# Score matmuls of two query tiles issued as one burst, with the second tile's PSUM banks read one and two steps later

## The chip, the core and the metric

The kernel runs on one core of one Trainium2 chip. The metric is the device time of one execution in microseconds (us). Before the change the median of three runs is 1856.72 us (1854.34 to 1858.67). A difference of 0.2% (3.7 us) is about what a measurement of this kernel can tell from no change.

Engines are named as the profile names them: PE is TensorE (PEld is its weight load), DVE is VectorE, ACT is ScalarE, POOL is GpSimd, SP is SyncE, which only issues DMAs here (SPq in the timeline).

## The reference

Inputs are `q`, `k`, `v` of shape (8 batches, 8 heads, 576 rows, 64), and the weights `moe_w_ch1` (512 x 2048) and `moe_w_ch2` (2048 x 512), all float32.

```python
scores = scale * np.matmul(q, k.transpose(0, 1, 3, 2))          # 576 x 576 per head
kth = np.partition(scores, -32, axis=-1)[..., -32:-31]          # 32nd largest of each row
scores = np.where(scores >= kth, scores, -1e9)
attn = softmax(scores); attn_out = attn @ v
x = attn_out.transpose(0, 2, 1, 3).reshape(8, 576, 512)
u = x + np.real(fft(fft(x, axis=1), axis=2))                    # FNet mix
un = (u - mean(u)) / sqrt(var(u) + 1e-6)                        # over the 512 channels
out = u + np.maximum(un @ w_ch1, 0) @ w_ch2
```

## The kernel before

**Work units.** Two heads of a batch make a pair, so there are 32 pairs, four to a batch (`NPB = 4`). A pair has nine items, numbered r = 0 to 8 here: `IN_PAIR = [(0, 0), (0, 1), (1, 0), (1, 1), (4, None), (2, 0), (2, 1), (3, 0), (3, 1)]`, each a query tile t of 128 rows and a head e. Item 4 holds the two heads' last 64 rows together. The 288 items follow each other; item i is worked on in step i of one long loop, which is written out when the kernel is built. Within an engine the instructions run in the order in which this loop issues them, and engines meet only at semaphores. The loop goes through the items as a software pipeline. In step i

- PE makes the scores of item i + 3 (`scores`), ACT copies them from PSUM to a tile `S`;
- DVE finds the 32 largest of each row (`top_ops`: four MAX8 and three MATCH_REPLACE8 of 128 x 576), the last two rounds of item i and the first two of item i + 1;
- POOL makes two bounds from them (`nt`, L434); one step later ACT and POOL form the mask (`mask`, L452 and L455), ACT takes the exponential (`expo`, L463);
- two steps later ACT splits the result into 16-bit planes (`plane`, L476), and SP writes them to DRAM (L489, L492); SP reads them back transposed into a tile `PT` (`turn`, L510), and `attend` (L568) multiplies `PT` with v on PE: the first three tiles of a pair in the step of the next pair's r = 0, the other two in that of its r = 3.

This way through DRAM (`by_dma`) is taken in pairs 4 to 30 except pair 7. In the first three pairs of each such batch the attention output is turned by DMA as well (`out_by_dma`).

**Scores of one tile, both heads.** An item of head 0 brings both heads' scores. With D = 64 the two heads lie on partitions 0 to 63 and 64 to 127, so the two matmuls `sp` (L401, 64 rows, 512 keys) use different row halves of PE. The last 64 keys of both heads come from one more matmul of the whole array, `sp_t` (L371), against a small tile `kt`. ACT empties these with two copies of 128 x 512 (L404) and two of 128 x 64 (L375, called tail copies here). In the trace a float32 matmul is two MATMUL instructions, so a tile's scores are four `sp` and two `sp_t` MATMULs. In a step whose item i + 3 has r = 2, 5 or 7 the scores are the first PE work of the step; for r = 0 they are the last of the step's listed work. Steps for r = 1, 3, 6 and 8 have no scores.

**PSUM.** Eight banks: `ps_s` two (tag "sp", the `sp` matmuls), `ps_t` two (tag "tp": `sp_t` and the transposes `prep` of q and k, L308), `ps_o` one, `ps_m` three (the MLP and the Fourier matmuls). Tiles of one tag take its banks in turn, so a `tp` tile waits until ACT has emptied the one before the last.

**What else PE does.** The Fourier mix of a finished batch (`yp` L789, `mp` L846 and L850, `tpu` L915) and its MLP in units of about 2 us: `hp` (L1000, first layer), `cp` (L1027, L1066) and, from the second batch on, a product with seven instead of eight block products (`cv`, `cw`, L1197), which needs sums of hidden blocks from POOL (L1142) and other parts of w2 fetched by SP in the middle of it (`bring`, L943, 512 KB each). A planner spreads these units over the steps: `level` finds a common step length, and after each listed piece of a step `some` issues units while `room`, the step's share less `fixed_cost(i)`, allows it. So `fixed_cost` moves MLP units, with their DMAs and POOL sums, between steps, and does not change their number.

```python
t += {0: 1.04, 1: 0.3, None: 0.9}[items[i + 3][2]]
if by_dma(i + 3) and items[i + 3][2] is not None:
    t += -0.3 if items[i + 3][2] else 0.3
```

## Time and profile before

| | us |
|---|---|
| median of three runs | 1856.72 |
| lowest, highest | 1854.34, 1858.67 |
| the profiled execution, its own time | 1856.44 |
| its span (what the profile shows) | 1854.0 |
| PE busy | 1685.3 (91%) |
| DVE busy | 1569.5 (85%) |
| ACT busy | 1299.3 (70%) |
| POOL busy | 942.7 (51%) |

The span is 2.4 us shorter than the execution's own time. The last MAX8 starts at 1645.8 us; what follows is the end of the last batch, in which PE does the Fourier mix and the MLP. DVE begins pair 20 at 1034.3 us and pair 24 at 1232.7 us: a whole batch in the middle takes some 198 us, of which DVE is busy in 190 and PE in 195.

A timeline line reads: start, duration, engine, line, operation, output <- inputs, tensor types, and how many instructions were merged into it; in brackets the idle time of the engine before it and what ended that.

### The profile page before, as it was taken

Reading aid. Unit: us, or ns where it says so; the run is one execution under the profiler, and the core shown is the slowest. Engines: PE = TensorE matmul, PEld = TensorE weight load, DVE = VectorE, ACT = ScalarE, POOL = GpSimd, SP = SyncE. Lnnn points to the kernel's source line nnn. Section 1 sums busy time; section 2 is a strip of 40 time slices with the busy share of each in tenths; the row PEclk is TensorE's granted clock in tenths of the full one; section 3 lists DMA queues with packets and bytes.
Section 4 is the critical chain, followed back from the end, with each engine's and each line's share of the span. In section 5 each row is a group of like instructions: output and inputs, shape, how many; then the busy total and the mean of one; then the engine's idle time right before and its main releaser. Section 6 shows DMA issues by size and latency. Waiting matters only on the chain.

```text
span 1854.0 us, 26945 instructions
## 1 busy us (share of the span) xinstructions
PE 1685.3 (91%) x8029; PEld 1077.7 (58%) x8029; DVE 1569.5 (85%) x3247; ACT 1299.3 (70%) x3116; POOL 942.7 (51%) x1341
## 2 busy tenths in 40 slices
PE   5676699789899899999999999999999999999999
PEld 3343365356455665557565765667565756676677
DVE  7999989888989999998999999999999899834010
ACT  6878659567698777877798788877887778642100
POOL 4768744454654565446654566355645554350012
PEclk8778799889899999999999999999999999999999
DMA  5334116761467955679557955687567745630051
GB/s 169 105 89 114 26 42 175 184 175 45 114 147 172 242 152 135 152 192 220 120 152 169 253 138 141 155 233 182 121 158 207 210 116 151 167 90 6 6 173 57
DMA packets 562609, 262.24 MB, mean 141 GB/s; under 512 B 433568, under 2 KB 552480, under 8 KB 562464
## 3 DMA queue, kind: packets, MB, share of 16 engines
q1 hardware_dynamic: 561696, 260.32, 54.8%
q8 instruction: 64, 1.05, 0.2%
q14 instruction: 81, 0.66, 0.1%
q10 hardware_dynamic: 768, 0.21, 0.0%
HBM read 93.63 MB, written 90.93 MB: 100 GB/s over the span
## 4 chain that ended last, share of the span: by engine, by line
PE 54%; DVE 13%; POOL 10%; ACT 9%; issue 6%; DMA 6%; SPq 2%; POOLq 0%; DVEq 0%
PE hp L1000 19%; PE cp L1027 6%; DVE m L425 6%; PE o L568 6%; DVE wk L427 6%; PE sp L401 4%; POOL wk L455 4%; PE cv L1197 3%; PE cw L1197 3%; PE yp L789 3%; PE cp L1066 2%; DMA PT<-planes 2%; ACT wk L452 2%; DMA planes<-wk 2%; PE sp_t L371 1%
## 5 line engine op out<-in xcount | busy, mean ns | idle before, releaser
L455 POOL TENSOR_TENSOR wk<-S,wk 128x576 f32<-128x576 f32 x288 | 407.7, 1416 | 495.6 <-ACT wk L452 490.7
L425 DVE MAX8 m<-wk 128x8 f32<-128x576 f32 x864 | 627.2, 750 | 6.6
L1000 PE MATMUL hp<-unT,w 128*128 128x256 f32 (+1 forms) x2048 | 525.6, 410 | 4.9 <-ACT unT L918 3.6
L1000 PEld LDWEIGHTS hp<-unT,w 128*128 128x128 f32 x2048 | 383.5, 192 | 114.1 <-issue 9.4
L427 DVE MATCH_REPLACE8 wk<-m,wk 128x576 f32<-128x576 f32 x576 | 427.7, 742 | 0.0
L476 ACT COPY wk<-S 128x576 uint16<-128x576 uint16 x468 | 289.8, 671 | 0.0
L452 ACT ACTIVATE wk<-S,nt 128x576 f32<-128x576 f32 x288 | 223.5, 776 | 84.5 <-POOL nt L434 83.0
L1027 PE MATMUL cp<-w,hT 128*128 128x512 f32 x512 | 234.6, 599 | 0.0
L425 DVE MAX8 m<-S 128x8 f32<-128x576 f32 x288 | 213.9, 743 | 24.0 <-ACT S L375 24.0
L463 ACT ACTIVATE S<-wk,nt 128x576 f32<-128x576 f32 x234 | 184.9, 790 | 52.0 <-POOL wk L455 50.8
L1004 ACT ACTIVATE hT<-hp 128x320 f32<-128x320 f32 (+1 forms) x256 | 103.2, 412 | 161.3 <-PE hp L1000 160.3
L427 DVE MATCH_REPLACE8 wk<-m,S 128x576 f32<-128x576 f32 x288 | 213.7, 742 | 0.3 <-issue 0.3
L568 PE MATMUL o<-PT,v 128*64 128x256 f32 (+3 forms) x1440 | 196.3, 417 | 7.6 <-DMA PT<-planes 5.5
L401 PE MATMUL sp<-kT,qT 64*128 64x512 f32 (+1 forms) x528 | 170.5, 674 | 12.9 <-ACT means L1391 5.7
L404 ACT COPY S<-sp 128x512 f32<-128x512 f32 (+1 forms) x264 | 141.8, 587 | 30.6 <-PE sp L401 29.9
L568 PEld LDWEIGHTS o<-PT,v 128*64 128x64 f32 x1440 | 115.1, 154 | 82.1 <-issue 23.1
L1027 PEld LDWEIGHTS cp<-w,hT 128*128 128x128 f32 x512 | 94.1, 193 | 90.4 <-issue 89.7
L1142 POOL TENSOR_TENSOR hT<-hT 128x512 f32<-128x512 f32 x64 | 81.0, 1272 | 117.9 <-ACT hT L1004 77.3
L1197 PE MATMUL cw<-w,hT 128*128 128x256 f32 x448 | 107.0, 388 | 13.8 <-ACT ct L1167 7.4
L434 POOL TENSOR_TENSOR nt<-m,cc 128x2 f32<-128x2 f32 x288 | 59.9, 208 | 115.0 <-DVE m L425 110.1
L371 PEld LDWEIGHTS sp_t<-kt,qT 128*128 128x128 f32 x320 | 51.2, 195 | 113.5 <-issue 67.2
L1197 PEld LDWEIGHTS cw<-w,hT 128*128 128x128 f32 x448 | 83.4, 192 | 31.4 <-ACT ct L1167 9.7
(162 smaller groups left out, 2129.7 us busy)
## 6 DMA issues: line engine op xcount, KB each, us to landing
planes<-wk SPq DMA_DIRECT2D x208, 288.0 KB, 2.8
w<-w_parts SPq DMA_DIRECT2D x82, 512.0 KB, 4.9
space<-in_moe_w_ch_dram SPq DMA_DIRECT2D x32, 512.0 KB, 3.6
nat<-in_q_dram SPq DMA_DIRECT2D x128, 64.0 KB, 2.3
v<-in_v_dram SPq DMA_DIRECT2D x64, 128.0 KB, 3.2
out_dram<-x SPq DMA_DIRECT2D x32, 256.0 KB, 2.6
nat<-in_k_dram SPq DMA_DIRECT2D x62, 128.0 KB, 3.2
planes<-wk SPq DMA_DIRECT2D x52, 144.0 KB, 2.6
```

The costliest lines, as they stand in the source:

```text
L401: nc.tensor.matmul(sp[r], lhsT=qT[hd, q_cols], rhs=kT[hd, :], start=True, stop=True)
L404: nc.scalar.copy(out=s_t[r, keys], in_=sp[r])
L425: ops.append(lambda src=src, m8=m8: nc.vector.max(out=m8, in_=src))
L427: ops.append(lambda src=src, m8=m8: nc.vector.match_replace(w, m8, src, NEG))
L452: nc.scalar.activation(out=w, in_=Ssb[i], func=AF.Relu, scale=-FAR, bias=Nt[i][:, 1:2])
L455: nc.gpsimd.tensor_tensor(out=w, in0=Ssb[i], in1=w, op=ALU.subtract)
L463: nc.scalar.activation(out=Ssb[i] if by_dma(i) else w, in_=w, func=AF.Exp, bias=Nt.pop(i)[:, 0:1], accum_out=den_t[pair % 3][:, c:c + 1],)
L476: nc.scalar.copy(out=words[:, half, :], in_=src[:, half, :])
L568: nc.tensor.matmul(o[D * e:D * (e + 1), c0:c1], lhsT=vv[:, c, e, :], rhs=pt[:, NF if c == NF else (NF + 1) * e + c, c0:c1], start=(c == 0) ...
L1000: nc.tensor.matmul(hp[:, 0:w], lhsT=w1[:, dt, P * it:P * (it + 1)], rhs=unT[:, dt, 0:w], start=(dt == 0), stop=(dt == NDT - 1),)
L1027: nc.tensor.matmul(cp, lhsT=hT[:, it, P * n:P * (n + 1)], rhs=w2[:, it, :], start=(it == 0), stop=(it == NIT - 1),)
L1197: nc.tensor.matmul(dst, lhsT=h()[a][:, kc, :], rhs=rhs_of(kc), start=start and kc == 0, stop=kc == NK - 1, skip_group_check=True,)
```

## The change

In pairs that go through DRAM, two tiles' score matmuls are issued together: r = 0 with r = 2, and r = 5 with r = 7. `burst` issues four `sp` matmuls (eight MATMULs): both heads of the first tile into the two `ps_s` banks, both heads of the second into the two `ps_t` banks. ACT copies the first tile's two banks at once, and the second tile's with `fetch` one and two steps later, behind that step's plane copies. The `sp_t` matmuls and tail copies stay in their steps: for r = 5, 2 and 7 as the first PE work of the step, for r = 0 behind the Fourier work. The burst is the last listed piece of its step, with part of the step's MLP units behind it. `fixed_cost` counts 2.4 us for a burst step (2.1 for the burst and 0.3 for `sp_t`), 0.3 for the second tile's step.

The first two tiles of a pair are burst only if the pair before also goes through DRAM: 24 such bursts, and 26 of the second kind. The fetched `S` tile of the second tile is now allocated one step earlier than before. The output that is turned by DMA is in both kernels.

```diff
+    def in_burst(i):
+        if not (0 <= i < N and by_dma(i)):
+            return False
+        r = i % PER_PAIR
+        return r >= 5 or (r < 4 and pair_by_dma(i // PER_PAIR - 1))
+
+    held = {}
+
+    def burst(i):
+        pair, t, _ = items[i]
+        for n, pool, tag in ((0, ps_s, "sp"), (2, ps_t, "tp")):
+            t = items[i + n][1]
+            for h in range(2):
+                hd = slice(D * h, D * (h + 1))
+                sp = pool.tile([P, NF * P], F32, name=f"sp_{i + n}_{h}", tag=tag)
+                nc.tensor.matmul(
+                    sp, lhsT=qT_of[pair][hd, P * t:P * (t + 1)], rhs=kT_of[pair][hd, :],
+                    start=True, stop=True,
+                )
+                held[i + n + h] = sp
+        for h in range(2):
+            fetch(i + h)
+        return 2.1
+
+    def fetch(i):
+        if i not in held:
+            return
+        if i not in Ssb:
+            Ssb[i] = attp.tile([P, S], F32, name=f"S_{i}", tag="S", bufs=6)
+        keys = slice(TAIL, S) if items[i][2] else slice(0, NF * P)
+        nc.scalar.copy(out=Ssb[i][:, keys], in_=held.pop(i))
...
     def scores(i, part):
-        if part == 0:
+        if part == 0 or in_burst(i) and i not in Ssb:
...
     def fixed_cost(i):
-            if by_dma(i + 3) and items[i + 3][2] is not None:
+            if in_burst(i + 3):
+                t = t - 1.04 + {0: 2.4, 5: 2.4, 2: 0.3, 7: 0.3}[(i + 3) % PER_PAIR] if items[i + 3][2] == 0 else t - 0.3
+            elif by_dma(i + 3) and items[i + 3][2] is not None:
                 t += -0.3 if items[i + 3][2] else 0.3
...
         last_scores = []
-        if PER_BATCH < j < N and j % PER_PAIR == 0 and by_dma(j):
+        if in_burst(j) and e == 0:
+            fixed.append(lambda: scores(j, 1) if j % PER_PAIR else 0.0)
+            if j % PER_PAIR in (0, 5):
+                last_scores.append(lambda: burst(j))
+        elif PER_BATCH < j < N and j % PER_PAIR == 0 and by_dma(j):
             fixed.append(lambda: 0.0)
             last_scores.append(lambda: scores(j, 0) + scores(j, 1))
...
-        if e is None and j < N:
+        if j < N and (e is None or in_burst(j) and j % PER_PAIR == 0):
             fixed.append(lambda: scores(j, 1))
...
         plane(i - 2, 0)
         plane(i - 2, 1)
+        if j % PER_PAIR in (1, 2, 6, 7):
+            fetch(j + 1)
         run(i, "convert")
```

## The prediction

> **What bounds the kernel now.** I read the page's totals, then the busy times batch by batch, then the waits of DVE, then the timelines around single score pairs.

> ```profile
> span 1854.0 us, 26945 instructions
> PE 1685.3 (91%) x8029; PEld 1077.7 (58%) x8029; DVE 1569.5 (85%) x3247; ACT 1299.3 (70%) x3116; POOL 942.7 (51%) x1341
> ```

> The columns of a stretch are its length, busy PE, PEld, DVE, ACT and POOL, granted clock, DMA share, GB/s. The first is a whole batch (pairs 20 to 23), the second the end.

> ```profile
> 1034.00:1233.00 199.00, 194.91 (x953) 124.41 (x952) 189.96 (x391) 159.57 (x383) 110.24 (x167) 1.00 0.68 173
> 1622.00:1854.00 232.00, 220.55 (x1003) 165.42 (x999) 46.13 (x108) 46.47 (x117) 49.22 (x72) 0.99 0.22 67
> ```

> Two engines are nearly full at once: PE idles 4.1 us of a batch, DVE 9.0. From 530 us to the end of top-k DVE's two largest waits are these:

> ```profile
> DVE wk L427 <- DMA planes<-wk: 14.9, 4, 4.7
> DVE m L425 <- ACT S L375: 12.7, 6, 2.3
> ```

> So a batch from the fourth on loses about 3.7 us at its start, where DVE waits for a plane write that frees a `wk` buffer, and about 2.1 us at its third pair, where it waits for scores. PE time that is saved or lost counts as far as it moves these two, and in full in the last batch, which PE ends alone. In batches 2 and 3 (pairs 4 to 11) PE idles more (179 busy of 200 us from 440 to 640) and I count nothing there.

> **What a burst saves.**

> ```profile
> 1001.30 2.32 PE L1000 MATMUL hp<-unT,w 128*128 128x320 f32 x8
> 1003.55 1.13 PE L401 MATMUL sp<-kT,qT 64*128 64x512 f32 x4
> 1004.61 0.49 PE L371 MATMUL sp_t<-kt,qT 128*128 128x128 f32 x2
> 1004.94 2.32 PE L1000 MATMUL hp<-unT,w 128*128 128x320 f32 x8
> ```

> The two heads run side by side: four MATMULs of 512 columns take 1.06 us from their start to that of `sp_t`. In a stream a MATMUL of 512 columns takes 0.43 (16 `cp` from 1105.16 to 1112.12 less 0.1), so two passes are 0.86 and 0.2 is overhead: 0.1 for a weight load that nothing covers and 0.1 of drain behind. Eight `hp` need 8 x 0.269 = 2.15 and take 2.25 before the scores: 0.1 of drain in front. `sp_t` takes 0.33 behind `sp` and 0.23 alone in the `hp` stream (1052.14 to 1052.37): 0.1 for its load. Each entry and exit of the half-array form thus costs 0.2, a pair 0.4. A burst has one entry and exit for two tiles: 0.4 saved for items 0 and 2. For items 5 and 7 it is 0.2, since item 7's scores stand behind `o` (L568, also a half-array form), and `o` to `sp_t` drains as `o` to `sp` did. 24 x 0.4 + 26 x 0.2 = 14.8 us, 2.4 per whole batch. The number of instructions, copies and DMAs stays.

> **What it adds.** The second tile sits in the two `tp` banks that `sp_t` uses. The order of `tp` tiles at a burst is ..., `sp_t` of the first tile, head 0, head 1; with two banks in turn, head 1 cannot start before ACT has made the tail copies of this `sp_t`. In the built kernel 49 of the 50 fourth matmuls carry a wait on ACT. Behind it are queued, on PE, everything: the MLP units, `o`, the next `sp_t`. Today's scores wait for `ps_s` banks, long empty. So the price is how late ACT is. Pair 21, items 5 and 6:

> ```profile
> 1103.02 1.89 PE L401 MATMUL sp<-kT,qT 64*128 64x512 f32 x4 [0.43 <-ACT S L393]
> 1105.16 7.03 PE L1027 MATMUL cp<-w,hT 128*128 128x512 f32 x16
> ```

> ```profile
> 1105.18 0.43 ACT L375 COPY S<-sp_t 64x64 f32<-64x64 f32 x2
> 1108.33 1.08 ACT L404 COPY S<-sp 128x512 f32<-128x512 f32 x2
> 1109.29 0.35 ACT L375 COPY S<-sp_t 128x64 f32<-128x64 f32 x2
> ```

> ACT comes to these copies 5.3 us after PE began the scores, held by POOL, which folds the last batch's Fourier input in these pairs. With the new order the tail copies come first, at 1108.33 + 0.35 = 1108.7. PE has its `sp_t` out at 1102.6, two `cp` (1.72) at 1104.4, the first tile at 1105.5, and would end the burst at 1106.3; head 1 now runs from 1108.7, alone, to 1109.6: 3.3 us lost. By the same reckoning pair 22's items 5 to 8 lose 2.8 (PE 1152.09, ACT 1157.87), pair 21's items 0 to 3 1.8 (1077.21, 1079.91), and pair 22's 2.7, of which 1.0 is today's wait of `mp` for `y`, so 1.7. The other bursts of a batch have ACT 1.2 to 2.3 us behind, just what the first tile needs, and lose nothing that shows (pair 20's second stands ahead of a wait of `o` for `PT`). The sum is 9.6, less 1.2 that today's pairs at these places lose to ACT (1.82 and 1.53 instead of 1.06). Each stall lets ACT catch up, so 8.4 is the upper end; the largest alone, 3.3, the lower. I take 7.0, since 20 to 50 us lie between them, in which ACT, waiting for PE's `yp`, slips too. PE per whole batch: 7.0 - 2.4 = +4.6.

> That banks can come back late shows today, in a `prep` behind a late tail copy:

> ```profile
> 722.03 0.48 PE L308 MATMUL tpk<-ident,nat 128*128 128x128 f32 x1 [3.19 <-ACT S L375]
> 720.90:727.70 6.80, 5.67 (x21) 3.08 (x23) 6.56 (x15) 6.76 (x19) 3.65 (x9) 0.50 0.38 115
> ```

> The 3.19 us stall is followed by 6.8 us at half clock; one of 2.39 at 691.52 by none. My stalls are cut in two by head 0, so I charge no clock, but a stall of over 3 us in one piece would cost some 3.4 us more.

> [...]

> **What is moved.** ACT's copies: in the second tile's own step one copy of 0.53 instead of two, the other a step earlier. At pair 22's first tile that helps:

> ```profile
> 1132.81 1.07 ACT L404 COPY S<-sp 128x512 f32<-128x512 f32 x2
> 1133.77 0.34 ACT L375 COPY S<-sp_t 128x64 f32<-128x64 f32 x2
> 1134.09 0.76 DVE L425 MAX8 m<-S 128x8 f32<-128x576 f32 x1 [2.13 <-ACT S L375]
> ```

> `S` is ready after tail and one copy, 0.75 instead of 1.18: 0.43 sooner, against PE and `y` later by 2 to 3, so this wait grows by 1 to 1.5 and does not vanish. MLP units slip by up to one (2 us) behind their steps, with SP's `bring` and POOL's sums. At the start of a batch this helps:

> ```profile
> 1038.34 0.57 SPq L489 DMA_DIRECT2D planes<-wk  x1
> 1039.00 1.73 SPq L943 DMA_DIRECT2D w<-w_parts  x3
> 1044.97 0.59 SPq L489 DMA_DIRECT2D planes<-wk  x1
> 1048.96 0.09 DVE L427 MATCH_VALUE_LOAD wk<-m,S 128x8 f32 x1 [3.00 <-DMA planes<-wk]
> ```

> In the changed order only one of the three `bring` stands ahead of the second plane write. That is worth 2 x 0.58 = 1.15 of issuing at least; with the wait of the v loads between (1.5) and a shorter queue (3.88 to land, median 2.8) 3.7 at most. I take 3.4: the three follow from the same two transfers.

> **The sum.** Per batch boundary (pairs 16, 20, 24, 28): +4.6 of PE, which carries the `bring`, less 3.4 = +1.2, four times +4.8. The last batch: +4.6, some of which PE's later idle takes back (11 us in the last stretch); bounds 0 and 4.6, I take 3.0. Together +7.8 on the profiled execution's 1856.4 (0.3 under the median): 1864 us. With the ends: 4 x (3.3 - 2.4 - 3.4) = -10 and 4 x (8.4 - 2.4 - 1.15) + 4.6 = +24.

> **Rivals.** (1) Faster: ACT is in time. If it makes the tail copies within about 3 us of `sp_t` (a `cp` pair and the first tile), nothing waits, PE gains 2.4 a batch, and DVE's two waits shrink by 0.43 + 2 and by 1.15 or more. For it: at the first scores of pairs 19, 20, 23 and 24 ACT's copies begin 1.2 us behind PE's start, at once. Against: four of a batch's eight bursts stand where they begin 2.7 to 5.8 behind. Price 2.4 in each of four to five batches: -10 to -12, 1845. (2) No change: stalls fall into idle that PE has anyway, and DVE paces the batches: 1857. (3) Slower by more: stalls in one piece at 3 us halve the clock, two in each of four batches, 3.4 each less some overlap: +20, 1878.

> **Chances.** Forecast (slower, 1858 to 1872) 0.42; rival 3, 0.18; rival 2, 0.13; rival 1, 0.27. A change under 0.2% (3.7 us) is about what a measurement cannot tell from none. Faster 0.27, same 0.13, slower 0.60. The range 1846 to 1881 leaves out some 0.1 on each side; the forecast's own is 1858 to 1872.

> **What would show it.** Right: waits of PE `sp` for ACT tail copies, some 7 us a batch, longest in the second bursts of a batch's second and third pair; plane waits of DVE shorter than 14.9. Right for the saving: eight MATMULs of `sp` in 1.9 us where ACT is level. Wrong: no such waits, or PE idle per batch not above 4.1; DVE's wait at the third pair gone.

## The result, and the profile after

The changed kernel takes 1902.37 us (median of four runs, 1897.17 to 1906.38) against 1856.41 us before (median of four): a ratio of 1.0246, 95% interval 1.0213 to 1.0278, slower. The profiled execution took 1906.38 us, the longest of the four and 49.9 more than the profiled one of before, and the readings of this section are of it. Line numbers after the scores function are those of before plus 35 (L427 is now L462); the burst is L351 and its copies L367.

The page's totals:

```profile
span 1904.5 us, 26975 instructions
PE 1705.6 (90%) x8029; PEld 1093.3 (57%) x8029; DVE 1570.0 (82%) x3247; ACT 1311.7 (69%) x3116; POOL 942.7 (49%) x1341
```

DVE has the same 1570 us of work, so its idle time grew by all of the loss. PE is busy 20 us longer, with the same number of matmuls (the granted clock is part of this, see below). The stretch of pairs 20 to 23 (columns as in the prediction), 213 us long now from first MAX8 to first MAX8 where it was 198:

```profile
1049.00:1261.00 212.00, 201.44 (x958) 128.72 (x956) 189.11 (x389) 162.65 (x385) 110.41 (x165) 0.98 0.66 162
```

PE now idles 10.6 us of it instead of 4.1, DVE 22.9 instead of 9.0. DVE's largest waits from 530 to 1640 us (pairs 11 to 30):

```profile
DVE wk L462 <- DMA planes<-wk: 19.6, 4, 5.3
DVE m L460 <- ACT S L367: 12.9, 5, 3.7
DVE x L677 <- PE tpx L674: 12.2, 5, 3.4
DVE rd L642 <- ACT rd L641: 11.6, 8, 3.1
```

The plane waits have grown from 14.9 to 19.6 us, and two waits that were small before (2.8 and 1.7 us) are now as large: `x` for `tpx` and `rd`, the last steps of an attention output. PE's two largest waits in the same stretch, where before it waited for no tail copy at a `sp` and 5.5 us for `PT`:

```profile
PE sp L351 <- ACT S L410: 13.6, 9, 2.4
PE o L603 <- DMA PT<-planes: 12.8, 5, 4.3
```

Where the loss is made, from the starts of the pairs on DVE: pairs 4 to 15 +12.9 us; the first, second, third and fourth pairs of the four batches from pair 16 on +19.6, +10.5, +5.2 and +1.6; the end +0.7.

**First pairs.** Pair 20 on SP, then PE, then DVE:

```profile
1076.78 1.15 SPq L978 DMA_DIRECT2D w<-w_parts  x2
1078.82 4.65 SPq L545 DMA_TRANSPOSE PT<-planes  x1
```

```profile
1085.68 4.07 PE L603 MATMUL o<-PT,v 128*64 128x256 f32 x20 [4.95 <-DVE m L460]
```

```profile
1090.29 0.18 DVE L642 RECIPROCAL rd<-rd 128x4 f32<-128x4 f32 x1 [3.12 <-ACT rd L641]
1093.87 0.42 DVE L677 TENSOR_TENSOR x<-tpx,rd 128x256 f32<-128x256 f32 x1 [3.41 <-PE tpx L674]
```

Two `bring` (L978) stand ahead of the read of `PT`, whose instruction holds SP's queue for 4.65 us; `o` waits 4.95 us (a MAX8 happens to end at that moment, but `o` reads nothing of it; the read landed at 1085.54, 0.14 us before `o` begins, as long before it as in the kernel before) and then takes 4.07 us; DVE, which has the `rd` and `tpx` of that `o` next in its order, stands 6.5 us. Before, one `bring` stood there, the read took SP 2.34 us, `o` waited 1.04 and took 2.38, and DVE lost 1.17.

**Second pairs.** Pair 21, items 5 to 8, where the prediction put the largest stall:

```profile
1129.90 2.33 PE L351 MATMUL sp<-kT,qT 64*128 64x512 f32 x6
1134.15 2.07 PE L351 MATMUL sp<-kT,qT 64*128 64x512 f32 x2 [1.92 <-ACT S L410]
1136.15 7.58 PE L1062 MATMUL cp<-w,hT 128*128 128x512 f32 x12
```

The burst takes 6.25 us. Its last two MATMULs wait for ACT's tail copy, and they and the first `cp` run at half speed, as the granted clock (third column from the end) of these four microseconds and the next says:

```profile
1134.00:1138.00 4.00, 3.85 (x4) 1.33 (x5) 3.93 (x10) 3.09 (x8) 3.11 (x5) 0.50 0.65 171
1138.00:1142.00 4.00, 4.00 (x8) 1.73 (x7) 3.93 (x7) 2.01 (x5) 4.00 (x8) 0.68 0.21 74
```

**Third pairs.** The S wait at pair 22 is 3.69 us, 2.13 before. **Where ACT is in time** (pair 20's first burst) eight `sp` take 1.92 us from their start to the next unit's:

```profile
1045.26 1.99 PE L351 MATMUL sp<-kT,qT 64*128 64x512 f32 x8
1047.18 1.99 PE L1232 MATMUL cw<-w,hT 128*128 128x256 f32 x8
```

### The profile page after: what moved, and what is told of

Read it like the earlier page. It is cut to its first block, busy times and chain, and to the rows that moved or that the text cites. A ratio compares the mean times of both kernels' runs of the same rounds, so it can differ in the third digit from the quotient of the medians.

```text
span 1904.5 us, 26975 instructions
## 1 busy us (share of the span) xinstructions
PE 1705.6 (90%) x8029; PEld 1093.3 (57%) x8029; DVE 1570.0 (82%) x3247; ACT 1311.7 (69%) x3116; POOL 942.7 (49%) x1341
## 5 line engine op out<-in xcount | busy, mean ns | idle before, releaser
L462 DVE MATCH_REPLACE8 wk<-m,wk 128x576 f32<-128x576 f32 x576 | 427.6, 742 | 0.0
L1062 PE MATMUL cp<-w,hT 128*128 128x512 f32 x512 | 247.7, 625 | 0.0
L603 PE MATMUL o<-PT,v 128*64 128x256 f32 (+3 forms) x1440 | 202.2, 427 | 19.7 <-DMA PT<-planes 12.8
L462 DVE MATCH_REPLACE8 wk<-m,S 128x576 f32<-128x576 f32 x288 | 213.6, 742 | 0.3 <-issue 0.3
L351 PE MATMUL sp<-kT,qT 64*128 64x512 f32 x400 | 131.9, 640 | 23.3 <-ACT S L410 22.9
L367 ACT COPY S<-sp 128x512 f32<-128x512 f32 x200 | 112.8, 593 | 23.1 <-PE sp L351 19.6
L1232 PE MATMUL cv<-w,hT 128*128 128x256 f32 x384 | 93.3, 392 | 9.3 <-DMA w<-w_parts 4.2
```

Source lines behind the costliest of these rows:

```text
L351: nc.tensor.matmul(sp, lhsT=qT_of[pair][hd, P * t:P * (t + 1)], rhs=kT_of[pair][hd, :], start=True, stop=True,)
L367: nc.scalar.copy(out=Ssb[i][:, keys], in_=held.pop(i))
L462: ops.append(lambda src=src, m8=m8: nc.vector.match_replace(w, m8, src, NEG))
L603: nc.tensor.matmul(o[D * e:D * (e + 1), c0:c1], lhsT=vv[:, c, e, :], rhs=pt[:, NF if c == NF else (NF + 1) * e + c, c0:c1], start=(c == 0) ...
L1062: nc.tensor.matmul(cp, lhsT=hT[:, it, P * n:P * (n + 1)], rhs=w2[:, it, :], start=(it == 0), stop=(it == NIT - 1),)
L1232: nc.tensor.matmul(dst, lhsT=h()[a][:, kc, :], rhs=rhs_of(kc), start=start and kc == 0, stop=kc == NK - 1, skip_group_check=True,)
```

## The experiments

Three parts of the change could each cost: the tp bank under the fourth matmul (theory P), the numbers in `fixed_cost`, which move the MLP units (theory U), and the place of the scores of r = 5, now at the end of their step (theory O). Ratios are against the kernel before, on the same chip. Each trace shows one execution; among those of its kernel it was the longest in e9, the shortest in e6 and e17, so that a difference of a few us between two traces is not told from chance.

**One part at a time.**

e1_costs_only: in the kernel before, nothing but the new branch of `fixed_cost`.

```diff
+            if in_burst(i + 3):
+                t = t - 1.04 + {0: 2.4, 5: 2.4, 2: 0.3, 7: 0.3}[(i + 3) % PER_PAIR] if items[i + 3][2] == 0 else t - 0.3
```

> The kernel before with only the changed numbers in fixed_cost: no burst, every tile's scores where they were. Theory P (the 46 us are made by the tp bank: the fourth matmul waits for ACT's tail copies): nothing happens, 1853 to 1860 us. Theory U (the planner's new numbers push MLP units about 1 us later in the steps of r = 0 and 5, and with them the masks, the planes and PT at a batch's start): most of the loss is here, 1880 to 1900. Theory O (the scores of r = 5 now end a step instead of beginning it): nothing, 1853 to 1860.

1905.55 us, 1.0248 (1.0217 to 1.0279): as slow as the changed kernel, without one burst. But it is slow in another way. Its waits of DVE from 530 us on:

```profile
DVE x L1162 <- POOL x L1176: 54.8, 6, 11.5
```

Here the planner spends 1.06 us too little in one step and too much in another, and DVE stands up to 11.5 us in an addition of a product (L1162) whose other half POOL has yet to add. In the changed kernel that wait is 7.1 us over the same stretch. There is no wait for a plane write left in e1 at all. So the places of the units can cost this much, but this run is not a share of the changed kernel's loss.

e2_place_only: the first tile's scores where the burst stands, the second tile's in their own step, old numbers.

```diff
-        for n, pool, tag in ((0, ps_s, "sp"), (2, ps_t, "tp")):
+        for n, pool, tag in ((0, ps_s, "sp"),):
...
+            else:
+                fixed.append(lambda: scores(j, 0) + scores(j, 1))
```

> The changed kernel with the burst taken out: the first tile's scores stand where the burst stands (tail matmul early, the two heads last in the step), the second tile's scores are made in their own step as before, and fixed_cost has the old numbers. Theory P: no tp bank is taken, 1853 to 1862 us. Theory U: 1853 to 1865. Theory O: most of the loss is here, 1880 to 1900, and DVE's waits at the first pair of a batch are as in the changed kernel.

1867.03 us, 1.0033 (1.0017 to 1.0049). Theory O has about an eighth of the loss, if any (e11 below).

e4_old_costs: the changed kernel without the new branch of `fixed_cost`.

> The changed kernel with the old numbers in fixed_cost: bursts as they are, MLP units spread as before the change. Theory U: most of the loss goes, 1855 to 1875 us. Theory P: 1895 to 1910, the stalls stay. Theory O: 1895 to 1910.

1881.92 us, 1.0123 (1.0095 to 1.0150): half of the loss goes. A burst still reports its 2.1 us to the planner's running account (`carry`), so the units are not where they were.

e6_units_as_before: old numbers, and the account is told 1.04 at the burst and 1.04 again in the second tile's step. Every step then has the units of before.

```diff
-        return 2.1
+        return 1.04
...
+            again = 0.0 if j % PER_PAIR in (0, 5) else 1.04
-            fixed.append(lambda: scores(j, 1) if j % PER_PAIR else 0.0)
+            fixed.append(lambda: scores(j, 1) + again if j % PER_PAIR else 0.0)
```

> The changed kernel, but the planner is told that a burst costs what one tile costs (1.04) and that the second tile's scores cost 1.04 in their own step: every step then gets exactly the MLP units that it has in the kernel before. Bursts, tp bank and copies stay as changed. If the place of the units is what costs, and the bank hardly: 1850 to 1865 us. If the bank costs by itself: 1870 to 1890, with PE sp waiting for ACT S 7 us in pairs 20 to 23, as forecast.

1876.99 us, 1.0099 (1.0069 to 1.0129). The units' places make 1.5 points of the 2.5; 1.0 is left, with waits of `sp` for tail copies of the kind that was forecast (530 to 1640 us):

```profile
PE sp L351 <- ACT S L410: 20.1, 13, 3.3
```

**A bank that was no cure.** e3_tail_bank, e5_bank_old_costs, e7_units_bank and e8_units_bank_start take the tail matmul of a burst's first tile out of the tp banks and put it into one of the three `ps_m` banks:

```diff
-            if by_dma(i):
+            if in_burst(i) and i % PER_PAIR in (0, 5):
+                sp = bank(shape, name)
+            elif by_dma(i):
```

e3 is the changed kernel with it, e5 has the old numbers too, e7 the units of before, and e8 is e7 with the burst of r = 5 at the start of its step.

> The changed kernel with the tail matmul of each burst's first tile written to one of the three ps_m banks instead of a tp bank, so that the fourth matmul of a burst no longer waits for ACT's tail copies. Theory P: the loss goes and the saving of the burst shows, 1842 to 1860 us, no wait of PE sp for ACT S of over 1 us. Theories U and O: 1885 to 1900, since the waits of DVE at a batch's first pair stay.

> Both cures at once: the changed kernel with the tail matmul of each burst's first tile in a ps_m bank (no wait of the fourth matmul for the tail copies) and the old numbers in fixed_cost. If bank and numbers are two separate causes (alone each left +1.2 to +1.3% of +2.5%), the loss is gone: 1850 to 1866 us. If both cures work only by moving the MLP units, so that they are two names of one cause, one of them is enough and the second adds nothing: 1875 to 1885.

> As the kernel with the units of before, and the tail matmul of each burst's first tile in a ps_m bank. Against that one the difference is the bank alone. If the two causes add: 1845 to 1858 us, the burst's saving shows. If something third costs (the scores of r = 5 at the end of their step, the second tile's copies a step early): 1862 to 1885.

> As the last, and the burst of r = 5 begins its step, as the scores of r = 5 do in the kernel before. If the place in the step was worth the 0.33% that the kernel without bursts showed: 6 us less than the last. Otherwise the same within 3 us.

1884.35 us, 1.0133 (1.0105 to 1.0161); 1875.99, 1.0092 (1.0068 to 1.0116); 1881.95, 1.0102 (1.0066 to 1.0138); 1872.48, 1.0074 (1.0053 to 1.0095). Read alone, e7 beside e6 would say that the bank costs nothing. The waits of PE in e3 (210 to 1700 us) say why that is not so:

```profile
PE sp_t L408 <- ACT y L862: 16.0, 6, 3.7
PE sp_t L408 <- ACT unT L955: 7.0, 5, 2.1
```

The wait for a tail copy was exchanged for one for the Fourier mix's copies, which use the same three banks.

**A bank that was a cure.** The `ps_o` bank holds `o` (320 columns) or `tpx` (384) and has 128 of the 512 columns of its tile (`one_bank` below) free. With one lasting tile over that bank, the tail matmul of a burst's first tile fits beside them.

```diff
+    one_bank = ps_o.tile([P, 4 * P], F32, name="one_bank", tag="o")
...
+            if in_burst(i) and i % PER_PAIR in (0, 5):
+                sp = one_bank[:, 3 * P:4 * P]
...
-            o_of[pair, ch] = ps_o.tile([P, CW[0]], F32, name=f"o_{pair}_{ch}", tag="o")
+            o_of[pair, ch] = one_bank[:, 0:CW[0]]
```

e9_tail_room is the changed kernel with it, e10_units_room also has the units of before.

> The changed kernel with the tail matmul of each burst's first tile in the 128 columns that o and tpx leave free in the ps_o bank. It then waits for hardly anything, and the fourth matmul of a burst no longer for ACT's tail copies, without a ps_m bank being taken (the kernel that took one had 30 us of new waits of sp_t for ACT). The planner's numbers stay as changed. If the tp bank costs by itself: 1870 to 1885 us, or less than the 1.33% that the ps_m bank left. If the ps_m bank helped only by chance of timing: 1890 to 1905.

> The kernel with the units of before (+0.99%), and the tail matmul in the free columns of the ps_o bank. If the tp bank costs by itself, it falls by the 26 us of waits of PE sp for ACT S at the share that reaches the end, 5 to 12 us: 1860 to 1870. If PE's waits there are covered by other waits: no change, 1873 to 1880.

1874.48 us, 1.0082 (1.0058 to 1.0106), and 1857.33 us, 0.9999 (0.9985 to 1.0013). With e6 this makes a square:

| | tp bank as changed | tail in the free columns |
|---|---|---|
| planner as changed | 1.0246 | 1.0082 |
| units as before | 1.0099 | 0.9999 |

In the traces the order of PE's other 6957 MATMULs, those of the scores left out, is the same in e6 and e10 as before, and the same in e9 as in the changed kernel, so the rows and columns are what they are called. Each cause costs by itself (1.0 point the bank, 0.8 the places), together 2.46: 0.65 more than their sum, where the four intervals together leave some 0.5 open. With both away nothing is left of the loss, and nothing of the saving shows either, though PE has it. The cure has a wait of its own. The tail matmul now waits until ACT has copied `o` out of the same bank (e10, 530 to 1640 us):

```profile
PE one_bank L409 <- ACT ow L623: 17.4, 12, 2.0
```

What it takes away is the delay inside the bursts. From its first matmul to the unit behind it a burst takes 1.92 us where it waits for nothing; the 50 bursts take 55.7 us more than that in the changed kernel and 54.5 in e6, but 3.2 in e9 and 0.7 in e10 (time at half clock is counted in).

The page's totals of e10, and its pairs 20 to 23:

```profile
PE 1664.6 (90%) x8029; PEld 1077.2 (58%) x8029; DVE 1567.9 (84%) x3247; ACT 1308.0 (70%) x3116; POOL 941.8 (51%) x1341
1038.00:1238.00 200.00, 192.32 (x953) 124.68 (x954) 190.14 (x393) 161.26 (x383) 109.44 (x165) 1.00 0.70 173
```

PE is busy 20.7 us less than before in all, and 2.6 less in pairs 20 to 23, where the granted clock is 1.00 in both. In these 200 us it idles 7.7; DVE is busy the same 190. The second pairs of the four batches gain 4.1 us in all; the first pairs lose 3.8 and the third 4.2. Why these lose is open.

**Third causes that were none.** e11_units_room_start is e10 with the burst of r = 5 beginning its step; e12_not_at_start is e11 without bursts at a batch's start:

```diff
+        if hp == (0 if r < 5 else NPB - 1):
+            return False
```

> As the last, and the burst of r = 5 begins its step. If the place in the step costs what the kernel without bursts showed (0.33%): 6 us less than the last. The plane waits of DVE at the first pair of a batch stay at 6 to 7 us each if they come from PE being ahead with scores and so late with the product whose copy ACT must make before the masks.

> As the last, but no bursts where ACT waits for PE around a batch's start: the last pair's items 5 to 8 and the first pair's items 0 to 3 have their scores one tile at a time, as in the kernel before. If the plane waits come from the burst's extra PE work ahead of the products, they go back to 3.0 to 4.7 us, and the time falls by some 12 us against the last, to 1845 to 1858: faster than before by the saving of the remaining bursts. If they come from something else (the order of o and tpx, SP's queue), they stay at 6 to 7 and the time within 4 us of the last.

1857.70 us, 1.0003 (0.9988 to 1.0018), and 1858.65 us, 1.0006 (0.9995 to 1.0017). The place in the step is worth nothing here. (e8 lies 9.5 us under e7, but e7's executions run from 1872.59 to 1886.13 us.) My reading that the bursts' early PE work makes the plane waits falls too: without those bursts the four waits are 6.2, 4.4, 4.9 and 4.9 us, with them 5.9, 5.0, 5.5 and 4.7. They do not need a burst either: in e2, which has none, they are 5.7, 5.9, 6.0 and 6.2.

**Why the places cost.** e13_before_unit_late holds one unit back around five batch starts in the kernel before; e14_before_unit_early has one more there, e15_room_unit_early the same in e10, e16_changed_unit_early in the changed kernel (+1.75 instead of -1.75 in these three).

```diff
         room = step_us - carry - fixed_cost(i)
+        if 3 * PER_PAIR + 3 <= (i - 8 * PER_PAIR) % PER_BATCH or (i - 8 * PER_PAIR) % PER_BATCH <= 4:
+            room += -1.75 if 11 * PER_PAIR < i < 29 * PER_PAIR else 0.0
```

> The kernel before, no bursts, with one MLP unit (1.75 us) held back from the step of r = 3 in a batch's last pair to that of r = 4 in the next batch's first pair, at five batch starts (pairs 12, 16, 20, 24, 28); after that the planner catches up. The units then stand in the last steps of pair 19 and the first of pair 20 as in the changed kernel. Theory L (one unit late at a batch's start costs by itself): 3 to 6 us a batch in the first pair, 1868 to 1885 us. The forecast's own step (slipping shortens the plane waits by 3.4 a batch): 1843 to 1852. Theory E (uneven steps elsewhere): 1854 to 1860.

> The kernel before with one MLP unit made earlier in the same steps. Theory L in a straight line: 3 to 6 us a batch less, 1830 to 1845. If the kernel before stands at a best place, early costs as well: 1862 to 1880. Theory E: 1854 to 1860.

> The kernel with the units of before and the tail matmul in the free columns of the ps_o bank (no slower than before, with 20.7 us less of busy PE), and one unit earlier around the start of a batch. If the PE time that the bursts save can be turned into earlier products there, the plane waits shrink: 1840 to 1852. If places earlier than those of before cost by themselves: 1862 to 1875.

> The changed kernel, all as it is, with one unit earlier in those steps, so that at the start of pair 20 as many units are left as before the change (35 instead of 36). Theory L: the first pairs of the batches get back 3 to 6 us each, 1880 to 1892. Theory E: 1898 to 1906.

Late: 1862.27 us, 1.0027 (1.0009 to 1.0046); of the 7.5 us in its trace 5.0 lie at pair 12. Early: 1868.84, 1.0058 (1.0037 to 1.0079). Early in e10: 1867.72, 1.0056 (1.0040 to 1.0071). Early in the changed kernel: 1899.80, 1.0235 (1.0214 to 1.0256), which its interval does not tell from unchanged. Lateness as such is not it; both directions cost, each by another wait. With the unit late the plane waits do shrink, and others grow (e13, 530 to 1640 us; before: 14.9, 1.7, 1.4):

```profile
DVE wk L427 <- DMA planes<-wk: 9.8, 4, 3.2
DVE rd L607 <- ACT rd L606: 9.8, 9, 2.9
DVE x L1155 <- POOL x L1169: 7.0, 4, 2.9
```

With the unit early (e14) DVE waits for POOL (22.1 us in 4). In e16 the plane waits fall from 19.6 to 10.6 us and those for `rd` and `tpx` from 23.8 to 12.2, but that for POOL grows from 3.5 to 17.7, and the time stays. One candidate is left: which neighbour a moved unit meets. In e9, at pair 20, two `bring` stand ahead of the read of `PT`, in e10 one (SP's queue, first e9, then e10):

```profile
1066.18 1.16 SPq L984 DMA_DIRECT2D w<-w_parts  x2
1068.21 4.23 SPq L548 DMA_TRANSPOSE PT<-planes  x1
```

```profile
1059.18 0.55 SPq L984 DMA_DIRECT2D w<-w_parts  x1
1062.16 2.37 SPq L548 DMA_TRANSPOSE PT<-planes  x1
```

e17_room_no_bring and e18_units_room_no_bring leave the `bring` of that step out of e9 and e10.

```diff
+        if now[0] >= 12 * PER_PAIR and now[0] % PER_BATCH == 1:
+            return
         nc.sync.dma_start(out=dst, in_=scr[:, o, kcs, :])
```

> The kernel with the tail matmul in the free columns of the ps_o bank and the changed planner's numbers (+0.82%), without the bring transfers issued in the step of r = 1 of the first pairs 12, 16, 20, 24 and 28 (two of 512 KB each in most of them; the products there use old values of w2, so this part of the output is not the reference's). If they hold up the read of PT: o's wait for PT of 3 us at pair 20 goes, DVE's waits for rd and tpx at r = 5 of the first pairs (3.4, 5.4, 1.7 and 2.8 us) shrink to under 1, and the time falls by 8 to 13 us to 1859 to 1867. If the read of PT is late for another reason: 1870 to 1877.

> The same left out in the kernel with the units of before and the tail matmul in the free columns (as fast as before, one bring in that step in pairs 20, 24 and 28, two in pair 16). If only the second bring of that step holds up PT: 1853 to 1858, within 4 us of that kernel. If any transfer there costs, whatever the place of the units: 1845 to 1852.

e17: 1869.86 us, 1.0071 (1.0043 to 1.0099). The trace does what the theory says. The same read, in e17:

```profile
1062.37 2.32 SPq L548 DMA_TRANSPOSE PT<-planes  x1
```

`o` waits 0.93 us there instead of 3.18, and DVE's waits for `tpx` fall from 11.3 to 4.8 us. But the time fell by 4.6 us at the medians where 8 to 13 were expected, and the intervals of e9 and e17 overlap. (The two traces differ by more, 1877.8 and 1863.0 us, since one is of the longest and the other of the shortest execution.) e18: 1856.26 us, 0.9994 (0.9980 to 1.0008), no change, as expected of a step with one `bring`. So the second `bring` makes the read of `PT` late; its share of the 15 us that the places cost is open, as is the rest of them. Nor does a late read always cost: in e13 two `bring` stand there too at pairs 20, 24 and 28, the read holds SP for 3.6 to 4.2 us, and `o` waits 0.4 us at most.

No version beat the kernel before.

## Why the prediction was wrong

The forecast, 1864 us, had the direction and the first cause; the time lies 21 us above the range of 1846 to 1881. Step by step:

- **What bounds: right.** DVE paces. PE time counts only where it moves DVE. (The row of 12.7 us for `S` ends at 1600 us and not with the top-k; to 1640 it is 16.2 in 7. The four at the third pairs, which the argument uses, are 8.4 of either.)
- **The saving: right in size, nothing in the time.** 2.4 us a batch by the rows; 2.6 less busy PE in pairs 20 to 23 of e10. The prediction let it reduce the loss. In e10 PE is busy 20.7 us less and the time is 0.9999. PE does wait for ACT to empty PSUM (13.6 us at `sp` in the changed kernel, 17.4 at the tail matmul in e10), but no run here shows that this is what takes the saving; the engine that stayed full is DVE, by its top-k (busy 190 of the 200 us).
- **The wait for the tp bank: right in mechanism and, in pairs 20 to 23, in size; not all in place.** 7.0 us a batch was taken, between 3.3 and 8.4. In pairs 20 to 23 of the changed kernel the bursts take 7.1 us more than 1.92 each, 4.3 of it in pair 21's second burst, where 3.3 had been forecast; pair 22's two lose 0.9 and 0.7, where 1.7 and 2.8 had been, and pair 23's second 1.1, where nothing had been; pair 21's first loses none of its 1.8. The other batches from pair 4 on lose 3.4 to 14.6 each. Moving the tail matmul out of the tp banks is worth 1.0 to 1.64 points (e6 to e10, the changed kernel to e9), 18 to 30 us. What was set against this wait is the wrong part.
- **"My stalls are cut in two by head 0, so I charge no clock": wrong.** The window of 1134 to 1138 us above is at 0.50; the clock fell at 1133.71, inside a split stall with a last piece of 1.92 us. Cutting the stall in two did not help: in the 3.41 us before the clock fell PE was busy for only 1.85 (last section). Adding (1 - granted clock) over windows of 5 us from the start of pair 12 to that of pair 31 gives 3.4 us of lost clock before, 20.4 after, 10.2 in e6, 15.3 in e9 and 5.2 in e10. Rival 3 had this at 20 us. That 17 came is luck: its stalls of 3 us in one piece did not occur at `sp` (the longest wait there is 2.4), and the clock was lost behind waits of `o` for `PT` as well (0.50 from 1085.92 to 1089.34 us, behind the 4.95 us at pair 20). How much of it reached the time is not shown.
- **"I take 3.4" of relief for the plane waits: the step that failed most.** They grew by 1.2 us a batch (14.9 to 19.6). Two things were wrong. First, with the units of before the same waits of `wk` at pairs 16, 20, 24 and 28 are longer in every kernel with moved scores: 19.0 us in sum in e10, 20.4 in e12, 23.8 in e6 and in e2 (the trace names another releaser for some); why is open. Second, a shorter plane wait is not time gained. With the new numbers and no burst (e1) the relief is there in full, no plane wait is left, and with a unit late (e13) they fall by 0.9 to 1.5 us at pairs 20, 24 and 28; neither kernel is faster, since DVE waits elsewhere, 49.6 us for POOL in e1 (530 to 1640 us). I followed the three `bring` away from the plane write and did not ask what stands behind them at their new place. In the changed kernel it is the read of `PT`, and behind it `o`, `rd` and `tpx`: DVE's waits for the last two went from 4.5 to 23.8 us. The first pairs, which were to lose 1.2 us each, lost 4.9.
- **Pairs 4 to 15 at nothing: wrong**, +12.9 us, 7.3 of it at pair 6. With the units of before (e6) these pairs lose 0.7 in all, with the changed places and the cured bank (e9) 5.8: half of it needs both. PE's idle time did not cover them.
- **"This wait grows by 1 to 1.5" at the third pair: right in three of four**, 2.13 to 3.69 at pair 22 and as much at 26 and 30; at pair 18 it fell from 2.23 to 1.44.
- **The range** added the ends of terms as if each could move alone. Its upper end had no term for waits that arise at a new place, and none for two causes that cost more together than apart (0.8 and 1.0 points alone, 2.5 together); rival 3 was held to exclude the forecast.

## What to carry to other kernels

In an order tuned by hand or by a planner, the cost table is part of the change: build the new order with the old costs first, so that work moved by the planner and work moved by the edit can be told apart. Where one engine paces, as DVE does here, time saved on another is worth nothing until it reaches a wait of the first (e10: 20.7 us of PE, time 0.9999), and a transfer followed away from one queue neighbour must be followed to the next (here the read of `PT`, 2.34 us on SP's queue before and 4.65 after). A cure that borrows another bank is no test until its own waits have been read (16.0 and 7.0 us in e3).
